# Four sequence-matrix blocks split on TensorE, and a re-ordered half-step plan, in an attention + Fourier kernel on one core

## The chip, the core and the metric

The kernel runs on one core of a Trainium2 chip. The metric is the device time of one execution in microseconds (us). The engines are named as in the profile: PE is TensorE's matmul row and PEld its weight loads, DVE is VectorE, ACT is ScalarE, POOL is GpSimd, and SP is SyncE, which here only issues DMAs.

## What is computed

Four layers over one sequence of S = 2048 rows of D = 640 numbers, each added to its input: attention, Fourier mixing, attention, Fourier mixing. The reference, cut to what matters (`idx` is the row minus 0, 2, ..., 14, and negative rows are masked):

```python
def _A_ref(x, wqkv, wo):                      # 32 heads of 20
    qkv = (x @ wqkv).reshape(B, S, 3, H, Dh)  # -> q, k, v
    kg, vg = k[..., idx, :], v[..., idx, :]   # 8 rows per query, 2 apart
    logits = einsum("bhsd,bhswd->bhsw", q, kg) * scale
    attn = softmax(where(mask, logits, -1e9))
    o = einsum("bhsw,bhswd->bhsd", attn, vg)
    return o.reshape(B, S, D) @ wo
def _B_ref(x, seq_re, seq_im, hid_re, hid_im):
    a, b = x @ hid_re.T, x @ hid_im.T
    return seq_re @ a - seq_im @ b
x = x + _A_ref(layernorm(x), wqkv, wo)
x = x + _B_ref(layernorm(x), ...)
x = x + _A_ref(layernorm(x), wqkv, wo)
x = x + _B_ref(layernorm(x), ...)
```

All arrays are fp32. Since the matmuls take a rounded form (fp32r), every operand is split into a high part and a low part, `low = x - high`, and each product is the sum of three: high by high, high by low, low by high (`PASSES`).

## The kernel before

**Layers and pieces.** `layer_a` is an attention layer (called with 0 and 2; the text says first and second attention layer), `LayerB` a Fourier layer. The rows are permuted on the host, even ones first, and stand in four chunks (c = 0 to 3) of four tiles of 128 rows (j = 0 to 3). The attention layers also do a part of the Fourier layer behind them: the product of the sequence matrix's first block column with the normalized rows, `z_mm`, in sixteen blocks (block 4c + j needs tile j of chunk c), each in three thirds of five matmuls.

**Half-steps.** Heads are taken four at a time; a unit u (0 to 31) is four heads of one chunk, and each unit has two halves. One half is one half-step s, numbered from about -8 to 66. In half-step s = 2u + jp VectorE multiplies q with the windows of k (`qk_mul`, L518), GpSimd adds the two halves of each head's 20 products (L521), VectorE sums the remaining ten (`qk_red`, L531). A half-step in `whole` leaves GpSimd's addition out, and VectorE sums all twenty. Then follow the softmax pieces (`soft`, L546 to L556, in phases sA to sF), with `exp` on ScalarE (L539) between the subtraction sC and the sum sD; three half-steps after its `qk_mul`, VectorE multiplies with v (`av_mul`, L561), and GpSimd adds over the 8 rows (`av_tree`, L576 to L578).

**The plan.** Every call of a layer is entered in a plan under a half-step and a phase, and the plan is played half-step by half-step in the order of the phases in `ph`, one string for s < 48 and one for the rest:

```python
for s in range(gs[0], last + 1):
    for ph in C["ph"][s >= 48].split():
        for fn, args in plan.pop((s, ph), ()):
            fn(*args)
```

Each engine executes its own instructions in this written order, and a wait holds up all that follows on that engine. SyncE's DMA queue is such an order too. The numbers in CFG are half-steps: `gs` for the 64 groups of QKV matmuls, `wo` for the output projection, `z` for the thirds of `z_mm`, `ln` for the normalization, `t2`, `t3` for transposes of the attention output.

**What the change touches.**
- Sequence blocks. `c_load` loads block z (128x512) into a `stg` buffer, `c_hi` (L985) copies its high part on ScalarE, `c_lo` (L1001) subtracts on VectorE, `c_put` stores both for the second attention layer. `zla` is by how many half-steps a block is prepared earlier, `cring` the ring of its tiles, here `s3`, `s0`, `s2`.
- Transposes. `tp` enters one for tiles of x or of the attention output in four phases: `peT0` (`pc_pe`, L414, matmuls with the identity into a PSUM bank), `hi` (`pc_hi`, L418, ScalarE copies the rounded high part out), `peL` (`pc_sub`, L422, a matmul with minus the identity subtracts the high part in the bank) and `actL` or `loE` (`pc_lo`, L437, ScalarE copies the low part out).
- `q_load` (L488) loads a unit's q into a `qs` buffer two half-steps ahead; `q_copy` (L491) moves it on ScalarE into the PSUM tile `pq` that `qk_mul` reads. There is one `qs` buffer. `w_load` (L504) loads the windows of k and v.
- `qkv_mm` (L449), `qkv_evac` (L456, out of PSUM into a `stg` buffer) and `qkv_store` (L465, L466) make k, v and q and store them. `stg` has two buffers, shared with the blocks.
- `wo_mm` (L601) is the output projection into the banks `aux0` and `aux1`, `wo_add` (L237) adds its result to the residual on VectorE. `ln_hi` and `ln_lo` (L955, L959) split the normalized rows; `lnv` tells whether `ln_lo` is on VectorE (1) or GpSimd (0).
- `wqg` tells which low halves of the QKV weights (`split`, L212) GpSimd forms in the first layer.

Of the kernel before, what the change touches and what calls it, by code (L numbers as in the profile page):

```python
# [21 lines left out]
H = 32  # L22
# [14 lines left out]
CFG = {'cput': [1, 1, 1, 1, 1, 1, 1, 1, 1, 1, 1, 1, 1, 1, 1, 1],  # L37
# [12 lines left out]
 'run': [{'pre': [0, 0, 0, 0, 0, 0, 0, 1, 0, 0, 0, 4, 0, 0, 0, 0],  # L50
          'post': [1, 5, 4, 2, 3, 3, 2, 6, 3, 1, 0, 3, 1, 3, 3, 3],
          'y': [[6, 6, 6, 6, 6], [13, 13, 16, 16, 16]]},
         {'pre': [0, 0, 0, 0, 0, 6, 0, 0, 2, 0, 0, 0, 0, 0, 0, 0],
          'post': [0, 4, 4, 5, 0, 2, 1, 1, 0, 5, 6, 0, 5, 1, 6, 0],
# [5 lines left out]
         'ord': [[2, 0, 1, 3, 4, 6, 5, 7], [0, 2, 1, 3, 4, 6, 5, 7], [0, 2, 1, 3, 4, 6, 5, 7]],  # L60
         'out': [20, 24, 28, 32, 36, 40, 44, 46],
         'wo': [23, 23, 26, 27, 30, 30, 34, 35, 37, 38, 42, 43, 46, 47, 49, 49],
         'woph': 'pe2',
# [4 lines left out]
         'z': [149, 149, 151, 151, 151, 152, 152, 154, 155, 161, 163, 163, 170, 170, 170, 172, 173, 173, 174, 175,  # L68
               176, 176, 177, 178, 180, 182, 182, 182, 185, 185, 185, 186, 186, 188, 191, 191, 191, 191, 194, 195,
# [7 lines left out]
         'kvq': [1, 1, 0, 0, 0, 0, 0, 0, 0, 0, 0, 0, 0, 0, 0, 0, 0, 0, 0, 0, 0, 0, 0, 0, 0, 0, 0, 0, 0, 0, 0, 0],  # L77
# [12 lines left out]
         'whole': [33, 57],  # L90
         'lnv': [1, 0, 1, 1, 0, 1, 0, 0, 0, 0, 0, 0, 1, 1, 0, 0]},
# [4 lines left out]
         'ord': [[0, 2, 1, 3, 4, 6, 5, 7], [2, 0, 1, 3, 4, 6, 7, 5], [0, 2, 1, 3, 4, 6, 5, 7]],  # L96
         'out': [20, 25, 29, 32, 36, 41, 44, 46],
         'wo': [22, 23, 28, 28, 30, 31, 34, 35, 38, 39, 42, 43, 46, 47, 48, 49],
         'woph': 'z1',
         'ln': [42, 42, 44, 46, 52, 54, 55, 56],  # L100
         'w2': [52, 53, 54, 55],
# [49 lines left out]
def tile_layers(ctx: ExitStack, tc: tile.TileContext, x, wqkv, wo, cs, wre, wim, out):  # L151
# [175 lines left out]
    def layer_a(li, stats, handoff, prev):  # L327
# [376 lines left out]
        def prologue_first():  # L704
# [27 lines left out]
            for k in range(3):  # L732
                whi(k, nc.scalar)
# [3 lines left out]
            for i in range(2):  # L737
                xt_pe(0, 0, i, f"t{i}")
# [707 lines left out]
```

## Time and profile before

| | |
|---|---|
| three runs | 1776.55, 1783.21, 1781.76 us; median 1781.76 |
| profiled execution | 1776.27 us; span on the core 1774.5 us |
| mean granted TensorE clock | 0.995 |
| first attention layer | from the start to about 411 us |
| second attention layer | from about 876 to about 1281 us |
| the two Fourier layers | what lies between, and after, to the end |

A line of the busy times by stage names the stretch, its length, then for each engine the busy us and the count of instructions. A line of the waits reads: engine and what it was about to do, `<-` what it waited for, then us in total, times, longest. A line of the groups has line, engine, operation, output `<-` inputs, shape and count, then busy us and mean ns of one, then idle time before them. A line of the timeline has start, duration, and the same names, with the idle time before it in brackets.

### The profile page before, as it was taken

Reading aid. Unit: us, or ns where it says so; the run is one execution under the profiler, and the core shown is the slowest. Engines: PE = TensorE matmul, PEld = TensorE weight load, DVE = VectorE, ACT = ScalarE, POOL = GpSimd, SP = SyncE. Lnnn points to the kernel's source line nnn. Section 1 sums busy time; section 2 is a strip of 40 time slices with the busy share of each in tenths; the row PEclk is TensorE's granted clock in tenths of the full one; section 3 lists DMA queues with packets and bytes.
Section 4 is the critical chain, followed back from the end, with each engine's and each line's share of the span. In section 5 each row is a group of like instructions: output and inputs, shape, how many; then the busy total and the mean of one; then the engine's idle time right before and its main releaser. Section 6 shows DMA issues by size and latency. Waiting matters only on the chain.

```text
span 1774.5 us, 26375 instructions
## 1 busy us (share of the span) xinstructions
PE 1727.7 (97%) x8798; PEld 1503.3 (85%) x8798; DVE 1369.2 (77%) x2124; ACT 812.1 (46%) x1700; POOL 625.7 (35%) x577
## 2 busy tenths in 40 slices
PE   9999998899999999999999999999999999999999
PEld 6878987777888888888898889888788888888888
DVE  5899899977767768668639987898877677677673
ACT  5554644544445445445533434444534443443441
POOL 3799898970000000000019987898300000000000
PEclk9999999999999999999999999999999999999999
DMA  6786668868777687687647856688688776867761
GB/s 231 233 279 208 202 205 276 279 245 292 269 268 234 219 268 239 208 273 231 220 143 244 260 175 215 204 303 289 206 296 276 260 231 224 269 224 235 257 210 52
DMA packets 266312, 419.38 MB, mean 236 GB/s; under 512 B 22176, under 2 KB 146592, under 8 KB 265920
## 3 DMA queue, kind: packets, MB, share of 16 engines
q1 hardware_dynamic: 262976, 415.72, 70.9%
q10 hardware_dynamic: 3200, 1.97, 0.4%
q8 instruction: 70, 1.15, 0.3%
q14 instruction: 66, 0.54, 0.1%
HBM read 332.46 MB, written 85.14 MB: 235 GB/s over the span
## 4 chain that ended last, share of the span: by engine, by line
PE 71%; DVE 13%; DMA 9%; issue 3%; ACT 2%; POOL 1%; SPq 1%; DVEq 0%; ACTq 0%; POOLq 0%
PE m L449 19%; PE aux L1090 13%; PE t L1189 10%; PE m L1189 10%; PE pq L1189 5%; PE xt L1189 5%; PE aux L601 5%; DMA xc<-stg 3%; DVE pr L518 2%; DMA win<-cs_in 2%; DVE pr L561 1%; DMA win<-kvb 1%; DVE lg L531 1%; DVE stg L1155 1%; DVE s L1001 1%
## 5 line engine op out<-in xcount | busy, mean ns | idle before, releaser
L449 PE MATMUL m<-r,s 128*128 128x480 f32 x1920 | 434.5, 381 | 4.1 <-ACT s L437 1.7
L449 PEld LDWEIGHTS m<-r,s 128*128 128x128 f32 x1920 | 355.0, 188 | 58.2 <-ACT stg L456 3.3
L1090 PE MATMUL aux<-r2a,zo 128*128 128x320 f32 x768 | 226.0, 309 | 0.0
L1182 ACT CAST r<-win 128x512 fp32r<-128x512 f32 x242 | 147.5, 621 | 171.2 <-DVE win L1218 84.8
L576 POOL TENSOR_TENSOR pr<-pr 128x640 f32<-128x640 f32 x126 | 209.2, 1660 | 31.3 <-DVE pr L561 30.0
L518 DVE TENSOR_TENSOR pr<-pq,win 128x1280 f32<-128x1280 f32 x128 | 189.8, 1483 | 35.4 <-ACT pq L491 17.1
L521 POOL TENSOR_TENSOR pr<-pr 128x640 f32<-128x640 f32 x126 | 180.1, 1429 | 100.7 <-DVE pr L518 100.4
L1090 PE MATMUL aux<-pr,zo 128*128 128x320 f32 x704 | 207.9, 309 | 0.0
L1183 DVE TENSOR_TENSOR r<-win,r 128x512 fp32r<-128x512 f32 x242 | 162.8, 686 | 42.0 <-ACT r L1182 40.9
L561 DVE TENSOR_TENSOR pr<-pq,win 128x1280 f32<-128x1280 f32 x128 | 190.7, 1490 | 4.1
L259 POOL TENSOR_TENSOR stats<-stats,mhalf 128x1 f32<-128x1 f32 (+1 forms) x32 | 23.2, 724 | 465.8 <-ACT stats L253 465.8
L1189 PE MATMUL m<-r,r 128*128 128x512 f32 x600 | 153.0, 389 | 0.1
L1090 PEld LDWEIGHTS aux<-r2a,zo 128*128 128x128 f32 x768 | 144.2, 188 | 1.9
L1090 PEld LDWEIGHTS aux<-pr,zo 128*128 128x128 f32 x704 | 132.2, 188 | 2.1
L1189 PEld LDWEIGHTS m<-r,r 128*128 128x128 f32 x600 | 112.4, 188 | 23.6 <-DVE r L1183 0.5
L1189 PE MATMUL t<-r,r 128*128 128x512 f32 x492 | 132.0, 390 | 0.0
L1016 PE MATMUL m<-s,r 128*128 128x512 f32 x384 | 121.2, 402 | 8.9 <-DVE r L959 3.5
L1016 PE MATMUL t<-s,r 128*128 128x512 f32 x384 | 118.2, 396 | 2.2 <-DVE ot L1069 1.3
L577 POOL TENSOR_TENSOR pr<-pr 128x320 f32<-128x320 f32 x126 | 114.3, 907 | 9.9
L456 ACT COPY stg<-m 128x480 f32<-128x480 f32 x128 | 71.2, 556 | 90.6 <-PE m L449 74.8
L531 DVE TENSOR_REDUCE lg<-pr 128x64 f32<-128x640 f32 (+1 forms) x128 | 104.4, 815 | 7.3 <-POOL pr L521 7.0
L1189 PEld LDWEIGHTS t<-r,r 128*128 128x128 f32 x492 | 92.4, 188 | 19.8
(274 smaller groups left out, 3206.1 us busy)
## 6 DMA issues: line engine op xcount, KB each, us to landing
win<-cs_in SPq DMA_DIRECT2D x346, 256.0 KB, 4.1
r<-xc SPq DMA_DIRECT2D x240, 256.0 KB, 4.3
win<-kvb SPq DMA_DIRECT2D x96, 440.0 KB, 5.0
xa<-cs_in SPq DMA_DIRECT2D x120, 256.0 KB, 3.8
win<-kvb SPq DMA_DIRECT2D x64, 360.0 KB, 4.8
xc<-stg SPq DMA_DIRECT2D x40, 512.0 KB, 3.3
kvb<-stg SPq DMA_DIRECT2D x60, 320.0 KB, 4.1
xr<-xs SPq DMA_DIRECT2D x40, 320.0 KB, 4.9
```

The source lines that it names most:

```text
L449: nc.tensor.matmul(mt[g][:, : 3 * F], st[:, a, k], wq[q][:, b, k], start=n == 0, stop=n == 14)
L518: nc.vector.tensor_tensor(pr, q, wview(u, jp, 0, [[1, FE]]), op=ALU.mult)
L521: nc.gpsimd.tensor_tensor(pv[:, :, 0:10], pv[:, :, 0:10], pv[:, :, 10:20], op=ALU.add)
L531: nc.vector.tensor_reduce(rows(lgs[u], jp), pv.rearrange("p (a h) d -> p a h d", h=HE), axis=AX.X, op=ALU.add,)
L561: nc.vector.tensor_tensor(pr.rearrange("p j w (h d) -> p (j w) h d", d=DH), rows(lgs[u], jp).unsqueeze(3).to_broadcast([P, 2 * W, HE, DH]) ...
L576: g.tensor_tensor(pr[:, :, 0:4], pr[:, :, 0:4], pr[:, :, 4:8], op=ALU.add)
L577: g.tensor_tensor(pr[:, :, 0:2], pr[:, :, 0:2], pr[:, :, 2:4], op=ALU.add)
L1016: self.last = nc.tensor.matmul(self.z[t][k], self.xn[c][:, a, j, k * P : (k + 1) * P], self.ct[s][:, b], start=s == 0 and i == 0, stop=s = ...
L1090: self.last = nc.tensor.matmul(self.ym[e][:, :320], zt[(k, a, ri)][:, j2 * P : (j2 + 1) * P], w[:, e * 320 : (e + 1) * 320], start=(k, a, ...
L1182: nc.scalar.copy(hi, raw)
L1183: nc.vector.tensor_tensor(lo, raw, hi.bitcast(F32), op=ALU.subtract)
L1189: nc.tensor.matmul(bank, w(a, kb), hl[b], start=start and (a, b) == (0, 0), stop=stop and (a, b) == (1, 0),)
```

## The change

Four of the sixteen blocks (8, 9, 10 and 12, by `cpe`) are loaded in the first attention layer from a copy of the matrix that the host has transposed, 128x128 piece by piece. They go through the four phases of a transpose instead of `c_hi` and `c_lo`: TensorE transposes the pieces into `aux0` or `aux1`, ScalarE copies the high part out, TensorE subtracts it, ScalarE copies the low part out. The ring of block tiles in that layer gets a fourth tile, `wa`. `qs` gets a second buffer, `stg` a third.

The plan's numbers are set anew. In the first 48 half-steps sC now stands ahead of av0 (`av_mul`) in both layers; in the second layer `red1` also stands ahead of sD. Block copies and `ln_lo` have phases of their own (`clo`, `lnl`) instead of `misc`, and several thirds of `z_mm` move by a half-step or to another phase, in the first layer in front of the `peL` of half-steps 52, 57, 58, 59 and 61, in the second in front of those of 50, 52 and 59. `whole` gets two more half-steps in each layer. In the first layer two `ln_lo` move to VectorE, in the second one moves to GpSimd; eight instead of four weight splits are GpSimd's; five pairs of k, v and q stores are issued by ScalarE instead of two. The start of the first layer is written as a string of steps (`pro`), in nearly the same order. `lnx` and the calls of `z_late` change no instruction here.

By count, TensorE gets 16 transposes and 4 subtracting matmuls more, ScalarE 4 copies more, VectorE 4 subtractions of 128x512 fewer, GpSimd 4 first additions fewer. 

The diff, cut:

```diff
- 'bufs': {'xa': 2, 'qs': 1, 'stg': 2, 'xr': 1},
+ 'bufs': {'xa': 2, 'qs': 2, 'stg': 3, 'xr': 1},
- 'wqg': [0, 0, 0, 0, 0, 0, 0, 0, 1, 0, 0, 1, 0, 0, 0, 0, 1, 1, 0, 0],
+ 'wqg': [0, 0, 0, 0, 0, 1, 0, 1, 1, 1, 0, 0, 0, 1, 0, 0, 1, 1, 1, 0],
...
  first attention layer:
-         't2': [48, 48, 47, 48, 52, 52, 52, 51],
+         't2': [48, 48, 48, 48, 51, 51, 52, 51],
-         'kvq': [1, 1, 0, 0, ...],
+         'kvq': [1, 0, 0, 1, 0, ..., 1 at 16, 26 and 30],
-         'cring': ['s3', 's0', 's2'],
-         'zla': [0, 0, 0, 0, 0, 0, 0, 0, 0, 0, 0, 0, 0, 0],
-         'ph': ['peT0 pe dma evac hi z1 z0 peL pe2 fin red0 dma2 qk sA sB av0 sD sE red1 sC loE exp evacA actL actl '
-                'sF evacO av1 qc dmaw dmas misc dmac dmar pe3w pe3',
-                'peT0 dma hi evac z0 pe peL pe2 z1 fin red0 dma2 qk sA av0 sD sB red1 sE loE sC actL exp evacA actl '
-                'sF evacO dmac av1 qc dmas misc dmar dmaw pe3 pe3w'],
+         'cring': ['s3', 's0', 'wa', 's2'],
+         'cpe': [0, 0, 0, 0, 0, 0, 0, 0, 1, 2, 2, 0, 2, 0],
+         'zla': [0, 0, 0, 0, 0, 0, 0, 0, 0, 0, 1, 0, 1, 0],
+         'ph': ['peT0 pe dma evac hi z1 fin z0 peL pe2 red0 qk sA dma2 sB sC av0 sD sE red1 loE exp actl evacA sF '
+                'actL evacO av1 qc dmaw pe3w dmas misc lnl clo dmac dmar pe3',
+                'peT0 evac dma hi z0 peL pe pe2 z1 red0 fin dma2 qk sA av0 sD sB red1 sE loE sC actL exp evacA sF '
+                'evacO dmac dmar av1 qc misc lnl clo dmas dmaw pe3 pe3w'],
-         'whole': [33, 57],
-         'lnv': [1, 0, 1, 1, 0, 1, 0, 0, 0, 0, 0, 0, 1, 1, 0, 0]},
+         'whole': [7, 19, 27, 57],
+         'lnv': [1, 1, 1, 1, 0, 1, 0, 0, 0, 1, 0, 0, 1, 1, 0, 0]},
...
  second attention layer:
-         't3': [59, 58, 60, 61],
+         't3': [59, 58, 60, 60],
-         'ph': ['peT0 dma evac hi z0 pe peL pe2 z1 fin red0 dma2 sA qk sD sB av0 red1 sE sC loE exp evacA actL actl '
-                'sF evacO av1 dmaw dmas qc misc dmar pe3w pe3 dmac',
+         'ph': ['peT0 dma evac hi red0 pe z0 peL qk z1 fin sA sB pe2 red1 dma2 sD sE evacA sC av0 loE exp actL actl '
+                'sF evacO av1 qc dmaw misc lnl clo dmas dmar pe3w pe3 dmac',
-         'whole': [],
+         'whole': [51, 55],
...
             if first:
                 la = C["zla"][z]
-                at(t - 2 - la, "dmac", handoff.c_load, z)
-                at(t - 1 - la, "hi", handoff.c_hi, z)
-                at(t - 1 - la, "misc", handoff.c_lo, z)
+                if C["cpe"][z]:
+                    tp(t - 1 - la, "c", 0, z, 0, 4, f"aux{C['cpe'][z] - 1}")
+                    at(t - 2 - la, "dmac", handoff.ct_load, z)
+                else:
+                    at(t - 2 - la, "dmac", handoff.c_load, z)
+                    at(t - 1 - la, "hi", handoff.c_hi, z)
+                    at(t - 1 - la, "clo", handoff.c_lo, z)
...
+        def ct_load(self, s):
+            self.raw[s] = T([P, 512], "stg", bufs=CFG["bufs"]["stg"])
+            nc.sync.dma_start(self.raw[s], cst[:, s, :])
+
+        def ct_new(self, s):
+            self.ct[s] = T([P, 2, 512], self.c_tag(s), F32R)
+            return self.raw[s], self.ct[s].rearrange("p a (k f) -> p a k f", f=P)
...
+    cst = np.ascontiguousarray(cs[0].reshape(P, NST, 4, P).transpose(3, 1, 2, 0).reshape(P, NST, 512))
```

The numbers of `gs`, `ord`, `out`, `wo`, `ln`, `z`, `early` and `run` change in places too, mostly by one half-step.

More of the change, by code (lines that the diff above doesn't have):

```diff
@@ L116 @@
          'cring': ['s3', 's0', 's2'],
[L117 to L121 removed]
+         'cpe': [0, 0, 0, 0, 0, 0, 0, 0, 0, 0, 0, 0, 0, 0],
@@ L150, in tile_layers @@
 @with_exitstack
-def tile_layers(ctx: ExitStack, tc: tile.TileContext, x, wqkv, wo, cs, wre, wim, out):
+def tile_layers(ctx: ExitStack, tc: tile.TileContext, x, wqkv, wo, cs, cst, wre, wim, out):
     nc = tc.nc
@@ L402, in pc_pe @@
                     (xnT if kind == "x" else oT)[(c, j, 1) if kind == "x" else (c, j)] = T([P, 2, KD, P], tag, F32R)
-                src, st = (
+                if kind == "c":
+                    src, st = handoff.ct_new(j)
+                else:
+                    src, st = (
                         (xnT[(c, j)], xnT[(c, j, 1)]) if kind == "x" else (oo[(c, j // 2)][:, j % 2], oT[(c, j)])
@@ L408, in pc_pe @@
                 pb, todo = banks[bank]
+                assert not todo or (kind != "c" and todo[-1][0].offset != pb.offset + col)
                 todo += [(pb[:, col + i * P : col + (i + 1) * P], src[:, k * P : (k + 1) * P]) for i, k in enumerate(range(k0, k1))]
@@ L853, in layer_a @@
                 else:
-                    tp(C["t3"][j] if j < 2 else TA, "o", c, j, 0, 3, f"aux{j % 2}", 0, ("ot", "s1", "zo0", "zo1")[j])
+                    tp(C["t3"][j] if j < 2 else TA, "o", c, j, 0, 3, f"aux{j % 2}", 0, (["ot", "s1"] + [CFG["zor"][(4 + x) % len(CFG["zor"])] for x in range(2)])[j])
                     tp(C["t3"][2 + j] if j < 2 else 67, "o", c, j, 3, 5, "aux0" if j < 2 else "pq", 256 * (j % 2))
@@ L882, in layer_a @@
         assert len(thirds) == 42
+        late = {}
         for z in range(len(thirds) // 3):
@@ L894, in layer_a, with z_late @@
             for p in range(3):
-                at(*thirds[3 * z + p], handoff.z_mm, z, p)
+                if thirds[3 * z + p][0] > last:
+                    late.setdefault(thirds[3 * z + p][0], []).append((z, p))
+                else:
+                    at(*thirds[3 * z + p], handoff.z_mm, z, p)
+        def z_late(t):
+            for z, p in late.pop(t, ()):
+                handoff.z_mm(z, p)
         with tc.manual_schedule(engines=ENGINES):
@@ L929, in layer_a @@
             handoff.z_mm(15, None)
-        assert not plan, plan.keys()
+        assert not plan and not late, (plan.keys(), late)
         return nstats
```

120 lines of the change are left out of this document (67 added, 53 removed), and 14 rows, old and new, of the table CFG.

## The prediction

> **What bounds the kernel now.** I read the page first, then the busy time by stage, then the waits of TensorE, VectorE and SyncE's queue inside the two attention layers.
>
> ```profile
> span 1774.5 us, 26375 instructions
> PE 1727.7 (97%) x8798; PEld 1503.3 (85%) x8798; DVE 1369.2 (77%) x2124; ACT 812.1 (46%) x1700; POOL 625.7 (35%) x577
> PE 71%; DVE 13%; DMA 9%; issue 3%; ACT 2%; POOL 1%; SPq 1%; DVEq 0%; ACTq 0%; POOLq 0%
> ```
>
> TensorE is busy 97% of the span and carries 71% of the chain. Averages hide the stages, so next the busy time in stretches (PE, PEld, DVE, ACT, POOL, then the granted clock, the DMA share and GB/s):
>
> ```profile
> 60.00:276.00 216.00, 210.84 (x1090) 186.03 (x1090) 199.54 (x287) 115.93 (x290) 199.30 (x185) 1.00 0.71 228
> 276.00:340.00 64.00, 52.77 (x285) 45.69 (x283) 59.19 (x88) 31.99 (x81) 55.61 (x51) 0.95 0.82 283
> 340.00:386.00 46.00, 41.27 (x191) 34.52 (x192) 43.58 (x60) 19.39 (x44) 42.57 (x37) 0.93 0.84 293
> 386.00:411.00 25.00, 21.39 (x107) 17.80 (x105) 14.31 (x29) 13.32 (x30) 5.09 (x5) 0.93 0.57 195
> 411.00:917.00 506.00, 503.54 (x2557) 440.17 (x2558) 357.03 (x584) 242.97 (x457) 5.62 (x6) 1.00 0.72 240
> 917.00:1146.00 229.00, 226.82 (x1174) 201.58 (x1173) 199.06 (x284) 90.26 (x218) 192.28 (x177) 1.00 0.70 221
> 1146.00:1262.00 116.00, 109.25 (x586) 94.20 (x585) 103.36 (x157) 56.08 (x140) 100.63 (x88) 1.00 0.78 268
> 1281.00:1774.00 493.00, 488.72 (x2487) 426.57 (x2485) 343.12 (x557) 198.10 (x343) 0.00 (x0) 1.00 0.70 230
> ```
>
> The two transform layers (411 to 917 and 1281 to 1774) keep TensorE busy for all but 2.5 and 4.3 us; the change hardly touches them, and I give them nothing. In the first attention layer TensorE is full until 276 and then idles 11.2 us (64.00 - 52.77), 4.7 us and 3.6 us in the next three stretches, at a granted clock of 0.95 and 0.93. In just those stretches VectorE idles only 4.8 us of 64 and 2.4 us of 46, and GpSimd is nearly as full. So the first layer's late part is paced by the VectorE/GpSimd attention chain, and TensorE waits for its products. The second attention layer is TensorE's until 1146; then it idles 6.8 us to 1262. What the change can win lies here: 24.7 us of TensorE idle from 60 to 411 and 8.9 us from 917 to 1262, not the 3% of the whole.
>
> What TensorE waits for from 276 to 411, then what VectorE waits for (60 to 386, then 917 to 1262), then the longest wait of SyncE's queue in either layer:
>
> ```profile
> PE aux L422 <- ACT s L418: 4.0, 3, 2.9
> PE aux L414 <- POOL pr L576: 3.2, 1, 3.2
> PE m L1016 <- DVE r L959: 2.5, 1, 2.5
> PE aux L422 <- ACT ot L418: 1.7, 1, 1.7
> ...
> DVE pr L518 <- ACT pq L491: 6.8, 5, 3.6
> DVE lg L531 <- POOL pr L521: 4.0, 7, 0.8
> DVE pr L518 <- DMA win<-kvb: 2.3, 3, 0.9
> ...
> DVE pr L518 <- ACT pq L491: 7.1, 5, 2.7
> DVE lg L546 <- ACT pq L491: 5.8, 4, 3.0
> ...
> SPq L488 <- ACT pq L491: 43.1, 11, 5.9
> ...
> SPq L488 <- ACT pq L491: 37.5, 12, 6.0
> ```
>
> VectorE's largest wait in both layers is for `q_copy` (L491) on ScalarE, and SyncE's queue stands 43.1 and 37.5 us behind `q_load` (L488), whose single `qs` buffer is free only after that copy.
>
> **The change part by part, first layer.** The four low halves (blocks 8, 9, 10 and 12) leave VectorE. In the trace they are the 9th, 10th, 11th and 13th of the fourteen `c_lo` from `stg`:
>
> ```profile
> 348.04 3.51 DVE L1001 TENSOR_TENSOR s<-stg,s 128x512 fp32r<-128x512 f32 x2
> ...
> 355.64 0.72 DVE L1001 TENSOR_TENSOR s<-stg,s 128x512 fp32r<-128x512 f32 x1
> ...
> 368.67 0.81 DVE L1001 TENSOR_TENSOR s<-stg,s 128x512 fp32r<-128x512 f32 x1
> ```
>
> 3.51 + 0.72 + 0.81 = 5.0 us, all where VectorE paces (its idle there is 2.4 of 46 us): **-5.0**.
>
> In their place come, per block, four transposes and one subtracting matmul on TensorE, and one more copy out of PSUM on ScalarE; a `c_hi` that read `stg` now reads PSUM. The nearest rows:
>
> ```profile
> L414 PE MATMUL xt<-ident,xa 128*128 128x128 f32 x96 | 14.4, 272 | 0.0
> L422 PE MATMUL xt<-s,nident 128*128 128x512 f32 x24 | 9.7, 403 | 3.2 <-ACT s L418 3.2
> L1189 PE MATMUL m<-r,r 128*128 128x512 f32 x600 | 153.0, 389 | 0.1
> L437 ACT CAST s<-xt 128x512 fp32r<-128x512 f32 x24 | 14.1, 589 | 2.8 <-PE xt L422 2.8
> ```
>
> A transpose occupies TensorE for 14.4 / 96 = 0.15 us, sixteen for 2.4 us; a subtraction for between 153.0 / 600 = 0.26 and 9.7 / 24 = 0.40 us, four for 1.0 to 1.6 us. Together 3.4 to 4.0 us in half-steps 59 to 61, where TensorE has 4.7 us idle. Half on the path: **+1.8** (0 if the idle takes all of it, +4.0 if that idle is gone). The mean of one transpose in the same row, 272 ns, is start to end of overlapping instructions. The Trainium skill (TensorE: Matmul & The Clock Gate, Part 4) gives about 275 ns for a transpose in a kernel; priced one after another at that figure, sixteen would be an estimated 4.4 us and the sum 1.0 us worse. The group's busy time decides for 0.15. The four ScalarE copies are 4 x 0.59 = 2.4 us, and ScalarE is busy 19.39 of 46 us: at nothing, or 2.4 us if they stand ahead of an `exp`.
>
> Block 12's transposes add a wait: their bank `aux1` is the one that `wo_mm` of chunk 3 fills in half-step 60, and `wo_add` empties it only at the end of half-step 61, so everything on TensorE queues behind it.
>
> ```profile
> 353.98 4.56 PE L601 MATMUL aux<-r2a,ot 128*128 128x320 f32 x30
> ...
> 361.19 0.48 DVE L237 SCALAR_TENSOR_TENSOR xa<-aux,xa 128x320 f32<-128x320 f32 x1
> ```
>
> TensorE is through with that product at 358.5 and `wo_add`'s first half ends at 361.7: 3.2 us of stall if nothing else moved. But three of the four removed `c_lo` (4.2 us) stand ahead of it on VectorE, so I cost it at **0**; 3.2 is the price without that cover.
>
> The softmax subtraction now stands ahead of `av_mul` in the first 48 half-steps, so `exp`, which blocks ScalarE's queue, is fed one `av_mul` earlier and `q_copy`, last in that queue, comes sooner: of the 6.8 us I take 2: **-2.0** (0 to -6.8). The second `qs` buffer ends SyncE's stand at L488, so window loads go out earlier: **-1.5** of the 2.3 us for windows. What is late next on that queue is the stores' wait for their evacuation, which is unchanged. The third `stg` buffer unties the block loads from earlier `c_lo`; counted within these.
>
> Layer normalisation's low halves: two more on VectorE, two fewer on GpSimd. `whole`: four half-steps instead of two skip GpSimd's first addition. One of either kind:
>
> ```profile
> L959 DVE TENSOR_TENSOR r<-r,r 128x640 fp32r<-128x640 f32 x5 | 5.4, 1073 | 0.0
> L959 POOL TENSOR_TENSOR r<-r,r 128x640 fp32r<-128x640 f32 x11 | 17.3, 1571 | 0.0
> L531 DVE TENSOR_REDUCE lg<-pr 128x64 f32<-128x640 f32 x126 | 101.4, 805 | 7.3 <-POOL pr L521 7.0
> L531 DVE TENSOR_REDUCE lg<-pr 128x64 f32<-128x1280 f32 x2 | 3.0, 1476 | 0.0
> ```
>
> VectorE gets 2 x 1.07 and GpSimd loses 2 x 1.57 us; as both are full I take half: **+1.0**. Two reductions longer by 1.476 - 0.805 are +1.3 us, against the 4.0 us that VectorE waits for GpSimd's L521 in seven places of about 0.6 us, some of them in half-steps 7 and 19, now `whole`: **-0.3**. Four weight splits moved to GpSimd lie before 60 us and at nothing.
>
> Half-steps 52, 57, 58 and 61 now have a third of a sequence product, or one more, between TensorE's transposes and the subtraction that waits for ScalarE (the waits on L418 above, 4.0 + 1.7). That only fills idle time of an engine that follows the chain: it is counted as what lets TensorE keep up, at 0. Half-step 60 loses such a filler.
>
> First layer: -5.0 + 1.8 - 2.0 - 1.5 + 1.0 - 0.3 = **-6.0 us**.
>
> **Second layer.** No block moves. VectorE's 12.9 us of waits on L491 (7.1 + 5.8) shrink by the same reorder and buffer, but until 1146 TensorE is full (226.82 of 229), so the gain can only appear as less of its 6.8 us idle to 1262: **-3.0**. One transpose group no longer waits for a `wo_add` that follows it, and half-steps 50, 52 and 59 get fillers: **-1.0**. Two more `whole` (+1.3) and one low half off VectorE (-1.07): +0.2. Together **-3.8 us**.
>
> The sum is -9.8 us: 1776.3 us (the profiled execution: span 1774.5 and 1.8 around it) becomes 1766.5. The three runs shown stand at 1776.6, 1781.8 and 1783.2; the mean of all four is 1779.5, 3.2 above the profiled one. For the median of new runs I add that: about **1769 us**.
>
> **Rivals.** *Everything goes* (chance 0.24): all of the waits on L491 and for windows in the first layer (-9.1 instead of -3.5), the added matmuls wholly in idle time (0 instead of +1.8), and the second layer's 6.8 us idle gone (-7 instead of -3.8): 10.6 us better, 1759. For: the waits are named and the buffers are what they wait for. Against: TensorE is full until 276, so what VectorE wins earlier shows only if TensorE's next wait is for VectorE.
>
> *TensorE covers it* (0.16): the reorder moves who waits, both layers keep their pace, and only -5.0 + 4.0 + 1.0 remain: 1779, no change. For: 210.84 of 216 us. Against: 24.7 us idle in that layer.
>
> *TensorE's clock falls* (0.13, the slower one). Where TensorE stood still for 3.2 us, at 291 to 295, the granted clock was halved after it:
>
> ```profile
> 291.07 0.61 PE L1016 MATMUL t<-s,r 128*128 128x512 f32 x2
> 294.88 0.45 PE L414 MATMUL aux<-ident,zo 128*128 128x128 f32 x1 [3.21 <-POOL pr L576]
> ...
> 297.79 1.06 PE L1016 MATMUL m<-s,r 128*128 128x512 f32 x2
> ```
>
> Two matmuls take 0.61 us before it and 1.06 us after it. By the granted clocks of the stretches the loss is 0.05 x 64 + 0.07 x 46 + 0.07 x 25 = 8.2 us already. If the stall at half-step 61 (3.2 us) comes and the emptier queue at 51, two thirds of a product fewer than before, lengthens that one, halved stretches double (+8.2) and none of the -9.8 but the 5.0 arrives: -5.0 + 4.0 + 3.2 + 8.2 = +10.4, 1790. It decides as soon as block 12 waits over 3 us for `wo_add`. The Trainium skill (same page, Part 1) says that an idle window of about 3.4 us halves the clock, and Part 4 that transposes do not count as activity; by that rule this layer, with sixteen more, would lose more clock. The halved stretch after 3.2 us agrees.
>
> *It does not do what it says* (0.05): `q_load` still waits, now for the stores to `qb`, and the reorder is undone by ScalarE's queue: without -2.0, -1.5 and -3.0, 1776.
>
> **How the numbers follow.** The forecast has 0.42, 1762 to 1774 by its own bounds. About 0.5% is what a measurement of this kernel can tell from no change; around the mean of 1779.5 these are 1771 and 1788. Faster: 0.24 and 0.27 of the forecast = 0.51. Same: the other 0.15 of it, 0.16 and 0.05, less 0.04 for the slow ends of those two = 0.32. Slower: 0.13 + 0.04 = 0.17. The range reaches down to 1751, everything-goes with the 8.2 us of lost clock back as well, and up to 1788; left out is the clock case at its full price and what little lies below.
>
> **What would show it.** Right: VectorE's L1001 from `stg` x10 instead of x14, the end of the first layer's full VectorE stretch before 382 instead of at 386, the waits L518 on L491 halved, SyncE's L488 waits gone, and TensorE's idle from 276 to 340 under 9 us. Wrong: a TensorE wait over 2 us ahead of the block transposes, a granted clock under 0.93 there, or an unchanged end of the first layer near 411.

## The result, and the profile after

The changed kernel takes 1763.14 us (median of 4 runs, 1762.23 to 1763.97) where the kernel before takes 1779.97 (1776.55 to 1783.21): a ratio of 0.9906, with a 95% interval of 0.9884 to 0.9927. The profiled execution takes 1763.97 us (before: 1776.27), so the two traces differ by 12.3 us in their spans and the medians by 16.8: the profiled execution of before was among the fastest of its kernel. The forecast was 1769 us, and the time lies on the side that was forecast and inside the range; most of the reasons behind the forecast were not the ones that the chip shows.

The head of the page after: its span and the busy times.

```profile
span 1762.2 us, 26348 instructions
PE 1727.8 (98%) x8818; PEld 1507.3 (86%) x8818; DVE 1366.8 (78%) x2117; ACT 814.1 (46%) x1704; POOL 621.8 (35%) x576
```

TensorE's busy time is what it was (1727.7 before) although it has 20 matmuls more, and VectorE has lost no more than 2.4 us. The kernel is shorter because TensorE stands still less. The busy time in stretches (PE, PEld, DVE, ACT, POOL, granted clock, DMA share, GB/s):

```profile
60.00:276.00 216.00, 213.22 (x1101) 188.07 (x1100) 199.11 (x283) 113.58 (x283) 195.26 (x182) 1.00 0.69 225
276.00:340.00 64.00, 57.01 (x298) 49.21 (x297) 61.91 (x93) 35.65 (x86) 58.30 (x52) 0.95 0.93 327
340.00:386.00 46.00, 41.13 (x215) 35.23 (x214) 36.43 (x52) 18.75 (x45) 35.35 (x32) 0.96 0.64 225
386.00:411.00 25.00, 21.29 (x98) 17.34 (x99) 17.64 (x34) 15.30 (x34) 4.97 (x4) 0.93 0.62 208
411.00:917.00 506.00, 504.96 (x2577) 442.30 (x2576) 354.72 (x579) 239.73 (x453) 6.50 (x7) 1.00 0.74 241
1146.00:1262.00 116.00, 111.02 (x600) 96.11 (x599) 104.21 (x161) 57.33 (x143) 95.33 (x84) 1.00 0.80 274
```

TensorE's idle time from 276 to 340 is 7.0 us instead of 11.2, and VectorE and GpSimd are no longer full from 340 to 386: VectorE idles 9.6 of 46 us there instead of 2.4. To see where the 12.3 us come from, one point of the program is looked up in both timelines: the last four transposes of an attention layer, which start in the first and in the second layer at (start in us, duration; before first, then after)

```profile
388.50 0.60 PE L414 MATMUL pq<-ident,zo 128*128 128x128 f32 x4
1259.74 0.60 PE L414 MATMUL pq<-ident,zo 128*128 128x128 f32 x4
```

```profile
384.78 0.60 PE L425 MATMUL pq<-ident,zo 128*128 128x128 f32 x4
1248.80 0.60 PE L425 MATMUL pq<-ident,zo 128*128 128x128 f32 x4
```

and, as a point some 90 us into the second layer, the fourth set of transposes of x that it puts into the bank `xt`, before and after:

```profile
973.87 0.60 PE L414 MATMUL xt<-ident,xa 128*128 128x128 f32 x4
```

```profile
969.23 0.60 PE L425 MATMUL xt<-ident,xa 128*128 128x128 f32 x4
```

So the first attention layer gives 3.7 us (388.50 - 384.78), the way from there to the point in the second layer another 0.9 (4.6 in all at 969), the rest of the second attention layer 6.3 (10.9 in all at 1249), and what lies behind it 1.4. Each trace is one execution, and the runs of one kernel lie some us apart: such a difference is that of two executions.

The waits after: TensorE from 276 to 411, VectorE from 60 to 386, VectorE from 917 to 1262, SyncE's queue from 60 to 386 (us in total, times, longest).

```profile
PE aux L433 <- ACT s L429: 4.3, 2, 2.1
PE aux L425 <- POOL zo L589: 2.0, 1, 2.0
PE m L1055 <- DVE r L990: 1.7, 1, 1.7
...
DVE pr L529 <- ACT pq L502: 11.2, 11, 2.4
DVE lg L542 <- POOL pr L532: 1.7, 4, 0.8
...
DVE pq L563 <- ACT lg L550: 10.5, 6, 2.7
DVE pr L529 <- ACT pq L502: 3.7, 6, 1.4
...
SPq L476 <- ACT stg L467: 49.2, 13, 10.2
```

The wait of VectorE for `q_copy` (L491 before, L502 now) has grown in the first layer, from 6.8 to 11.2 us, and moved to `exp` (L550) in the second. SyncE's queue hardly stands at `q_load` any more (3.7 us); it stands 49.2 us at the stores of the evacuated pieces instead.

### The profile page after: what moved, and what is told of

Read it like the earlier page. It is cut to its first block, busy times and chain, and to the rows that moved or that the text cites. A ratio compares the mean times of both kernels' runs of the same rounds, so it can differ in the third digit from the quotient of the medians.

```text
span 1762.2 us, 26348 instructions
## 1 busy us (share of the span) xinstructions
PE 1727.8 (98%) x8818; PEld 1507.3 (86%) x8818; DVE 1366.8 (78%) x2117; ACT 814.1 (46%) x1704; POOL 621.8 (35%) x576
## 4 chain that ended last, share of the span: by engine, by line
PE 88%; DMA 4%; DVE 4%; ACT 2%; issue 1%; POOL 0%; SPq 0%; ACTq 0%; DVEq 0%
PE m L460 24%; PE aux L1129 15%; PE t L1228 10%; PE m L1228 10%; PE aux L612 6%; PE pq L1228 5%; PE xt L1228 5%; PE t L1055 4%; PE m L1055 4%; PE xt L1055 2%; DMA win<-cs_in 1%; DMA win<-kvb 1%; DMA stg<-cs_in 1%; PE t L425 1%; PE xt L425 1%
## 5 line engine op out<-in xcount | busy, mean ns | idle before, releaser
L587 POOL TENSOR_TENSOR pr<-pr 128x640 f32<-128x640 f32 x126 | 208.7, 1657 | 44.9 <-DVE pr L572 43.8
L532 POOL TENSOR_TENSOR pr<-pr 128x640 f32<-128x640 f32 x122 | 174.9, 1433 | 85.4 <-DVE pr L529 84.9
L1055 PE MATMUL m<-s,r 128*128 128x512 f32 x366 | 114.9, 402 | 6.2 <-DVE r L990 2.6
L1055 PE MATMUL t<-s,r 128*128 128x512 f32 x366 | 113.4, 398 | 2.3 <-DVE ot L1108 1.4
L1257 DVE TENSOR_TENSOR win<-win,win 128x512 f32<-128x512 f32 x109 | 74.8, 689 | 49.2 <-DMA win<-cs_in 47.8
```

The lines of the kernel that those rows point to most:

```text
L532: nc.gpsimd.tensor_tensor(pv[:, :, 0:10], pv[:, :, 0:10], pv[:, :, 10:20], op=ALU.add)
L587: g.tensor_tensor(pr[:, :, 0:4], pr[:, :, 0:4], pr[:, :, 4:8], op=ALU.add)
L1055: self.last = nc.tensor.matmul(self.z[t][k], self.xn[c][:, a, j, k * P : (k + 1) * P], self.ct[s][:, b], start=s == 0 and i == 0, stop=s = ...
```

## Experiments

Three theories stood against each other at first. By the prediction VectorE's path is shorter (the low halves, the softmax order, the earlier windows). By the second, TensorE's order in the two attention layers makes the gain (which thirds of a sequence product stand where TensorE would wait). By the third, the buffers make it. Each run was timed against the kernel before on the same chip, in five rounds; the ratios have 95% intervals.

**The buffers without the plan.**

```diff
- 'bufs': {'xa': 2, 'qs': 1, 'stg': 2, 'xr': 1},
+ 'bufs': {'xa': 2, 'qs': 2, 'stg': 3, 'xr': 1},
```

> The kernel before with two qs and three stg buffers and nothing else. VectorE-path theory: the waits for windows and half of those on q_copy go, 3 to 6 us below before, SyncE's waits at L488 under 10 us per layer. TensorE-order theory: within 2 us of before. Buffer theory: 10 us or more below.

Measured: 1772.23 us against 1781.38, 0.9954 [0.9943, 0.9966]. Two numbers give half of the whole gain. Which of the two it is, two more runs tell.

> The kernel before with one number changed: three stg buffers instead of two (qs stays at one). The stg ring holds the evacuated query/key/value pieces and the raw sequence-matrix blocks of the attention layers, but also the pairs of split halves that the Fourier layers store (L1151). In the kernel before VectorE waits there for the store to leave its stg buffer (L1153, 2.8 and 2.5 us near 482 and 1353 us) and TensorE then for ot (1.85 and 1.35 us over its pitch). Theory A (this ring is what the buffers bring): 3.2 us from these two places and 2 to 4 us in the attention layers, so 5 to 7 us faster, about 1775, and both Fourier stalls gone. Theory B (the prediction: the qs buffer is the one that frees the window loads, the stg buffer is a means): under 2 us, and the Fourier stalls stay.

> The kernel before with two qs buffers instead of one (stg stays at two). Theory A (the stg ring brings most of it): SyncE's wait at L488 goes, its queue then stands at the stores' wait for their evacuation (L465) instead, and the time moves by 0 to -3 us. Theory B (the prediction): the windows come earlier, -1.5 us in the first layer and as much of the second layer's idle, so -3 to -4 us, and the two Fourier stalls stay under both. If the two buffers alone each bring much less than both together (9.2 us), they gate one another on SyncE's queue.

The third `stg` buffer alone: 1772.19 against 1780.02, 0.9960 [0.9948, 0.9971]. The second `qs` buffer alone: 1779.13, 0.9993 [0.9984, 1.0002]. It is `stg`, and SyncE's long stand at `q_load` cost little or nothing (by the interval, its end lies between 2.8 us faster and 0.4 us slower): in the run with the third `stg` and a single `qs` the queue still stands there for as long as before, and the run is as fast as the one with both buffers within the intervals. In the run with the second `qs` alone that stand is gone and the queue stands at the next entry. Its trace reaches the first layer's last transposes 2.4 us earlier than before's (386.06), but of that 0.1 us is left at the point in the second layer (973.76). The waits of SyncE's queue from 60 to 386, `stg` run first, `qs` run second:

```profile
SPq L488 <- ACT pq L491: 42.1, 12, 5.9
SPq L465 <- ACT stg L456: 17.9, 10, 5.8
```

```profile
SPq L465 <- ACT stg L456: 55.6, 15, 6.2
```

Part of what `stg` gives lies where the prediction gave nothing. The Fourier layers put their split halves into the same ring (L1151) before they store them. In the kernel before VectorE waits there for the store to leave the buffer, and TensorE then for VectorE (waits from 411 to 917, then from 1290 to the end):

```profile
DVE stg L1153 <- DMA xc<-stg: 7.1, 6, 2.3
PE t L1189 <- DVE ot L1072: 1.7, 1, 1.7
...
DVE stg L1153 <- DMA xc<-stg: 9.9, 9, 2.3
PE t L1189 <- DVE ot L1072: 1.2, 1, 1.2
```

With the third buffer VectorE's wait is down to these (the second stretch from 1285 here, from where before has 10.4 us), and neither of TensorE's two rows is left:

```profile
DVE stg L1153 <- DMA xc<-stg: 3.1, 4, 1.6
...
DVE stg L1153 <- DMA xc<-stg: 3.1, 4, 1.1
```

TensorE's 2.9 us are gone in the changed kernel as well. The rest of the 7.8 us is not carried by any single wait in these traces, and the two traces end only 4.1 us apart (1774.5 and 1770.4): 1.4 us of it are there at the first layer's last transposes (387.09), 1.3 at the second's (1258.45), and 2.8 come behind those, where the last Fourier layer lies. The Trainium skill (Perfetto Trace Analysis, Optimization Strategy) says that the same gap coming again and again on the engine that should be saturated can mean that there is no room for the next tile, the number of buffers being one cause that it names. Here such a gap stood on VectorE, which is not saturated (busy 357 of 506 us), and a buffer more made it smaller (17.5 to 6.2 us from 411 to 917 and from 1285).

**The four blocks without the rest** (the kernel before with its own buffers and half-steps, but block 12 one half-step earlier, and the phases `lnl` and `clo` behind `misc` as in the changed kernel).

```diff
+ 'cpe': [0, 0, 0, 0, 0, 0, 0, 0, 1, 2, 2, 0, 2, 0],   # first layer
- 'cring': ['s3', 's0', 's2'],
+ 'cring': ['s3', 's0', 'wa', 's2'],
- 'zla': [0, 0, 0, 0, 0, 0, 0, 0, 0, 0, 0, 0, 0, 0],
+ 'zla': [0, 0, 0, 0, 0, 0, 0, 0, 0, 0, 0, 0, 1, 0],
- ... qc dmaw dmas misc dmac ...           # ph, here s < 48
+ ... qc dmaw dmas misc lnl clo dmac ...
```

> The kernel before with blocks 8, 9, 10 and 12 through TensorE (block 12 one half-step earlier, the ring with the tile wa), old plan and old buffers. VectorE-path theory: -5.0 on VectorE and +1.8 on TensorE, about 3 us below before. TensorE-order theory: no gain, 0 to 4 us above before, since the added transposes stand on the old plan without fillers and block 12 waits for wo_add. Buffer theory: within 2 us.

Measured: 1786.14, 1.0032 [1.0019, 1.0044], slower. The waits of TensorE from 276 to 411 show one for the load of the transposed copies into `stg`, which the kernel before does not have:

```profile
PE aux L425 <- DMA stg<-cst_in: 2.2, 2, 1.3
```

If the ring is what makes the blocks a loss, a third buffer ends it:

> The kernel before with the four blocks formed on TensorE, as in the run of the blocks alone (5.7 us slower than before there), and now with three stg buffers. Alone, the third stg buffer gave 7.8 us (1772.2 against 1780.0). Theory A (the blocks lost because a transposed copy holds its stg buffer until TensorE comes to its transposes; TensorE waited 2.2 us for the loads into stg): with the third buffer the loss is gone, 1771 to 1774. Theory C (the transposes and the extra bank cost TensorE themselves on the order of before): the loss stays, 1776 to 1779. The prediction (VectorE's pace, -5.0 + 1.8): 3 us faster than the third buffer alone, about 1769.

Measured: 1774.86, 0.9965 [0.9953, 0.9977], the same as the third buffer alone (0.9960) within the intervals, and that wait is down to

```profile
PE aux L425 <- DMA stg<-cst_in: 1.0, 2, 0.7
```

The loss is gone, and no gain comes in its place. But the two runs do more than move four blocks: with `lnl` and `clo`, VectorE does some additions of the output projection ahead of low halves of the normalization (near 256, 276 and 316 us). The run of the second layer's plan further down has this order in its first layer too, with both buffers and no block, and is later there than the run of the buffers alone (the last four transposes of the first layer, buffers alone first):

```profile
385.93 0.60 PE L414 MATMUL pq<-ident,zo 128*128 128x128 f32 x4
```

```profile
390.16 0.60 PE L425 MATMUL pq<-ident,zo 128*128 128x128 f32 x4
```

So how much of the loss of the blocks alone (4.8 us by the medians, 5.7 by the ratio, beside a wait of 2.2) is theirs, and how much that order's, isn't told by these runs, and neither is what the blocks are worth on the old order. The third question on the blocks is what they do inside the changed kernel:

```diff
- 'cpe': [0, 0, 0, 0, 0, 0, 0, 0, 1, 2, 2, 0, 2, 0],
+ 'cpe': [0, 0, 0, 0, 0, 0, 0, 0, 0, 0, 0, 0, 0, 0],
```

> The kernel after with the four blocks back on VectorE (c_hi from stg, c_lo from stg and s), all else as after. The prediction's step: +5.0 on VectorE, -1.8 on TensorE, so 3.2 us slower than after, about 1766. Theory A (the buffers and the order brought what the kernel after gained, and VectorE's and GpSimd's slack covers the four low halves now: VectorE idles 9.6 of 46 us from 340 to 386): within 1.5 us of after either way. Theory C (the blocks are a loss here too, as alone on the old order, where they cost 5.7 us): 3 to 6 us faster than after.

Measured: 1763.53, 0.9905 [0.989, 0.992], against 0.9906 [0.9884, 0.9927] with the blocks. The intervals alone would leave room for some 5 us either way, so the trace is asked: its stretch from 340 to 386, and the start of the last four transposes of the first layer.

```profile
340.00:386.00 46.00, 38.50 (x189) 32.43 (x189) 41.73 (x57) 17.97 (x42) 37.93 (x33) 0.93 0.68 236
```

```profile
384.80 0.60 PE L425 MATMUL pq<-ident,zo 128*128 128x128 f32 x4
```

The blocks do exactly what they say: with them VectorE has 5.3 us less to do in this stretch (36.43 against 41.73) and TensorE 2.6 us more (41.13 against 38.50). The layer gets to its last transposes at 384.78 with them and at 384.80 without, and at the two later points the traces are 0.2 us apart (969.23 and 1248.80 with, 969.04 and 1249.03 without). TensorE's waits for VectorE from 276 to 411 are 5.5 us with the blocks and 5.7 without, none of them for a block's low half. The work taken off VectorE came off an engine that did not pace, and what TensorE got was put into its own idle time: 7.5 us without the blocks, 4.9 with them.

**One layer's plan at a time**, both with the new buffers. In the first run the second layer's entries of `ly` and `run` are those of before; in the second run it is the first layer's, without the blocks and with the prologue of before. The old layer has the phases `lnl` and `clo` in both.

> The change in the first attention layer alone: the second layer has its old plan, both have the new buffers. VectorE-path theory (the prediction's): first layer -6.0 us and part of the second layer's -3.0 through the buffers, so about 7 us below before. TensorE-order theory (fillers and half-steps of the sequence thirds): the change's trace is 3.7 us ahead at the end of the first layer and 8.4 us more by the end of the second Fourier layer, so about 4 to 6 us below before. Buffer theory: nearly all of the 12 to 17 us, as the buffers serve both layers.

> The change in the second attention layer alone, with the new buffers in both layers; no block goes through TensorE. VectorE-path theory: -3.8 us of the second layer and 2 to 4 us through the buffers in the first, about 6 below before. TensorE-order theory: the second layer's fillers carry 6 to 8 us. Buffer theory: nearly all of the 12 to 17 us again.

Measured: 0.9942 [0.993, 0.9955] with the new first layer, 0.9938 [0.9926, 0.995] with the new second layer, against 0.9954 [0.9943, 0.9966] with the buffers alone. Each plan alone gives 2 to 3 us more, within the intervals; both together bring the ratio to 0.9906, 8.5 us (0.0048 of 1780) below the buffers. Whether the two add is not settled by the times: what is left over, some 3.5 us, is no larger than the intervals. The traces say where to look. Between the two points of the second layer 279.5 us pass with its new plan alone (975.94 to 1255.45), as in the changed kernel (279.6), and 287.0 with the buffers alone (970.12 to 1257.12): that layer's gain comes with its own plan. The old layers lose meanwhile, 4.2 us in the second run's first layer (390.16 against 385.93) and 2.3 us between the two points in the first run (289.3 against 287.0), so each plan looks smaller alone than it is.

**What in the plan counts.** First the fillers: the thirds of sequence products that stand between the second transposes and the subtraction that waits for ScalarE's copy. In the changed kernel's plan for half-steps 48 and later, in both layers, the phase `z0` goes behind `peL`. That takes out the new fillers and also those that the kernel before had.

```diff
-'peT0 evac dma hi z0 peL pe pe2 ...     # first layer
+'peT0 evac dma hi peL z0 pe pe2 ...
-'peT0 evac dma red0 z0 hi pe peL pe2 ...  # second layer
+'peT0 evac dma red0 hi pe peL z0 pe2 ...
```

> The kernel after with the thirds of sequence products (phase z0) back behind the second transposes' subtraction (peL) in the last half-steps of both attention layers, where the kernel before had most of them. The prediction counted these fillers at 0 in the first layer and -1.0 with another edit in the second. By the prediction: at most 1 us slower than after. Theory D (the fillers are what keeps TensorE running past ScalarE's copy): the waits of L433 on ScalarE's copy L429 come back, 2 to 5 us slower than after, 1765 to 1768.

Measured: 1769.77 (1766.0 to 1771.99), 0.9939 [0.9926, 0.9952], 6.6 us above the changed kernel (5.9 by the ratios, whose intervals just touch; no run of it is as fast as the slowest of the changed kernel). In the first layer (276 to 411) TensorE's waits of L433 for ScalarE's copies of `s`, `zo` and `ot` (L429) have grown from 4.5 us to the 8.4 us of three rows below, the wait for a bank that VectorE empties (L244) has grown from 1.3 us, and the last transposes come 7.0 us later:

```profile
PE aux L433 <- ACT s L429: 4.9, 4, 2.6
PE aux L425 <- DVE xa L244: 2.3, 1, 2.3
PE aux L433 <- ACT zo L429: 2.2, 1, 2.2
...
PE aux L433 <- ACT ot L429: 1.3, 1, 1.3
```

```profile
391.73 0.60 PE L425 MATMUL pq<-ident,zo 128*128 128x128 f32 x4
```

Then the softmax's place, back behind `av0` in the first 48 half-steps of both layers:

```diff
-'... qk sA dma2 sB sC av0 sD sE red1 loE ...   # first layer
+'... qk sA dma2 sB av0 sD sE red1 sC loE ...
-'... sE evacA sC av0 loE ...                   # second layer
+'... sE evacA av0 sC loE ...
```

> The kernel after with the softmax subtraction (phase sC) of the first 48 half-steps back behind av_mul (av0), in both layers. The prediction took 2.0 us in the first layer (0 to 6.8) and most of 3.0 us in the second for this and the buffer: 3 to 5 us slower than after, 1766 to 1768, and more wait of VectorE for q_copy (L502) than after's 11.2 us from 60 to 386. The other theory: in after's trace those waits are not smaller than before (11.2 against 6.8 us), and TensorE is full until 276 in the first layer and until 1146 in the second, which is where these half-steps lie; then the place is worth within 1 us of after, 1762 to 1764.

Measured: 1764.34, 0.991 [0.9897, 0.9922], 1.2 us above the changed kernel's median and not to be told from it. VectorE's waits for `q_copy` from 60 to 386 are no larger in the old place (11.2 in the new one):

```profile
DVE pr L529 <- ACT pq L502: 10.7, 9, 2.6
```

The traces leave room for a small gain by the new place. In the old one the first layer's last transposes come 4.0 us later (row below, against 384.78) and the second's 2.6 us (1251.41 against 1248.80); the spans end only 0.3 us apart, but the granted clock from 1262 to 1281 was 1.00 with the old place and 0.91 in the changed kernel.

```profile
388.81 0.60 PE L425 MATMUL pq<-ident,zo 128*128 128x128 f32 x4
```

Then more of what counted. Three thirds move one phase earlier, to `z0`: one each in half-steps 58 and 60 of the first layer, one in half-step 58 of the second.

```diff
- ... 173, 174, 174, 175, 175, 175, 176, 177, 181, 182 ...   # z, first layer
+ ... 173, 174, 174, 174, 175, 175, 176, 177, 180, 182 ...
- ... 171, 171, 173, 175, 176, 177 ...                       # z, second layer
+ ... 171, 171, 173, 174, 176, 177 ...
```

> The kernel after with three thirds of sequence products moved one phase earlier, ahead of the second transposes' subtraction: in the first layer one in half-step 58 (from phase z1 to z0, beside the two that are there) and the one of half-step 60 (z1 to z0), in the second layer one in half-step 58. In after's trace TensorE stands 2.3 us at each of the two places of the first layer and 0.7 us in the second, and a third of a product is about 1.4 us. Theory D (fillers ahead of ScalarE's copy are what the new order gains by): 1.4 + 1.4 + 0.7, up to 3.5 us faster than after, 1760 to 1762. The prediction (an engine that follows the chain has only its idle time filled): no change, 1763.

Measured: 1759.31 (1757.52 to 1760.97), 0.9874 [0.9859, 0.9889]. No run of it is as slow as the fastest of the changed kernel (1762.23), although the two intervals touch. It is the fastest version here. The wait for ScalarE's copy in the first layer is less than half of what it was (4.3), and the layer's last transposes come 2.4 us earlier:

```profile
PE aux L433 <- ACT s L429: 1.9, 2, 1.6
```

```profile
382.39 0.60 PE L425 MATMUL pq<-ident,zo 128*128 128x128 f32 x4
```

Of the 3.6 us between the two traces (spans 1762.2 and 1758.6) 1.9 are there at the second layer's last transposes (1248.80 and 1246.92), and all of it comes from the first layer: the third moved in the second layer changes nothing between its two points (279.57 and 279.55 us). The other 1.7 us come behind, where the granted clocks differ (last section).

At last, whether the third buffer and the new half-steps of the thirds make the change without the rest: the kernel before with `stg` 3 and the two `z` lists of after.

> The kernel before with two things of the change alone: three stg buffers, and the half-steps of the thirds of sequence products (the lists z of both layers) as in the kernel after, so that half-steps 57, 58 and 61 of the first layer have a third ahead of the second transposes' subtraction. No block on TensorE, one qs buffer, every other half-step as before. The third buffer alone stood at 0.9960 of before, the kernel after at 0.9906, the kernel after without its fillers at 0.9939. Theory D (the ring and the fillers are nearly all of it, and they add): 0.9960 less 0.0033, so 0.9925 to 0.993, about 1767. Rival E (fillers gain only where the rest of the half-steps' order is the new one, which has the copies and the loads of the blocks in other places): 0.995 to 0.997, 1773 to 1776, as the third buffer alone.

Measured: 1774.96, 0.9969 [0.9956, 0.9982], as the third buffer alone: the theory that fillers and ring add up fell. On the old order TensorE's waits of L422 for ScalarE's copies from 276 to 411 are 6.2 us before and already down to 1.8 with the third buffer alone, so there was little left to fill. With the new half-steps they are 2.6, GpSimd's last sums cost 5.1 (7.0 in two rows with the buffer alone), and a wait for a bank that VectorE has to empty comes new:

```profile
PE aux L414 <- POOL zo L578: 5.1, 3, 1.8
PE aux L414 <- DVE xa L237: 3.6, 1, 3.6
PE aux L422 <- ACT s L418: 2.1, 2, 1.2
```

A reading that no run shows by itself: a filler gains only where nothing else ends just behind it, and the new order is one in which the bank and the sums are nearly in time (1.3 and 2.0 us there).

## Why the prediction was right or wrong

The time was right: 1769 was forecast, 1763.14 came, inside the range; as a sum against its own execution -9.8 us were forecast and the traces show -12.3. Of the terms few held, and misses of both signs made up for each other.

- *First layer, -6.0.* The traces show -3.7; that of the buffers alone already shows -2.6 (385.93).
- *The low halves, -5.0 on VectorE and +1.8 on TensorE.* Both amounts of work came true (5.3 us off VectorE; the sixteen transposes were priced at 2.4 us, and their row after is below), and the time did not: the layer reaches its last transposes 0.02 us earlier than without them. The step that failed is "all where VectorE paces". VectorE is full there, but with 5.3 us taken off it TensorE's waits for VectorE are 5.5 us instead of 5.7, those for ScalarE the same 6.4, and only those for GpSimd fall (6.4 to 3.6), by about the work that TensorE gets. A full engine beside an idle TensorE was taken for the one that sets the pace. Besides, its busy time is in part waiting: a low half takes 0.68 us by itself, four 2.7, and the rest of the 5.0 was spent behind GpSimd's instructions (last section).

```profile
L425 PE MATMUL aux<-ident,stg 128*128 128x128 f32 x16 | 2.2, 272 | 0.0
```

- *The softmax's place, -2.0.* The wait that it was to shorten grew in the whole change (6.8 to 11.2 us), and the place does not set it (10.7 with the old one). In the time the place is worth 1.2 us and not told from nothing; one trace has more (4.0 us at the first layer's last transposes), so the mechanism failed and the size is open. The half-steps it touches lie where TensorE is full, which was what stood behind the rival *TensorE covers it*.
- *The second `qs` buffer, -1.5 and part of the second layer's -3.0.* 0.9993 [0.9984, 1.0002] alone. The stand of SyncE's queue at L488 is gone as forecast, but what it held up was not late. The stores' wait behind it was called unchanged; it grew from 18.9 us to 55.6.
- *The third `stg` buffer, "counted within these".* This is the largest miss: alone, on the old order, it gives 7.8 us, nearly half of the change. Only its use for the block loads was priced. That the Fourier layers take their staging from the same ring, where a store holds it, was not looked up; *Fourier layers: nothing* failed with it, if only by the 0.9 and 1.4 us that the traces of before and after show around those parts.
- *Fillers, at 0.* Their place is worth up to 6.6 us in the new order (with those that before had), nothing in the old one, and 3.8 us more with three further ones (1.9 in the traces without the last stretch, where the clocks differ). "An engine that follows the chain" was said to have only its idle time filled; here the same thirds otherwise stand behind the wait, on TensorE's own path, and the layer ends later.
- *Second layer, -3.8.* The traces show -6.3. `q_copy`'s 12.9 us of waits became 3.7 plus 10.5 at `exp`, so the named mechanism is not it. The fillers account for 1.9 of it: without them the two points of that layer are 281.5 us apart (rows below), with them 279.6 (969.23 to 1248.80). The remainder goes with the new order of that layer, as its plan alone shows (279.5 us), and was not taken apart.

```profile
977.37 0.60 PE L425 MATMUL xt<-ident,xa 128*128 128x128 f32 x4
...
1258.87 0.60 PE L425 MATMUL pq<-ident,zo 128*128 128x128 f32 x4
```

- *The stall at half-step 61 at 0, wq splits at 0, low halves of the normalisation and `whole` at +1.0 and -0.3.* Block 12's four transposes start at 358.11 us behind no wait, so the cover held. The others were not tried alone, so the sum of the first layer can't be followed term by term.
- *Rivals.* The clock stayed where it was (0.95, 0.96 and 0.93 in the three late stretches, 0.95, 0.93 and 0.93 before), although the layer has sixteen more transposes. By the Trainium skill (TensorE: Matmul & The Clock Gate, Part 4) these do not count as activity; the loss of clock that the rule would give did not come. *Everything goes* (1759) was nearer to the time than the forecast, for other reasons than its own. *It does not do what it says* had the worth of `qs` and of the softmax's place about right, but not its reason: `q_load` hardly waits any more.
- *What would show it.* Ten `c_lo` from `stg` instead of fourteen, SyncE's waits at `q_load` gone and TensorE's idle from 276 to 340 under 9 us (7.0) came true; the waits for `q_copy` halved and VectorE's full stretch ended before 382 did not (in the changed kernel it is busy 3.96 of the 5 us from 380 to 385). Three true signs stood beside a wrong cause: they showed that the edits had taken place, not that they paid.

How much of the 16.8 us is accounted for: 7.8 by the `stg` ring, if it is worth in the new order what it is in the old one (the changed kernel with two `stg` buffers was not run); nothing that could be told from 0 by the blocks and by `qs`; the other 9, by subtraction, by the new order of the two layers, in which the fillers' place, with those that before had, carries up to 6.6. Which edits of that order make the fillers work there and not on the old order is open.

## What to carry to other kernels

A full engine next to an idle TensorE is a suspect, not the bound: look at what TensorE's own waits name, and ask what frees that. Before a ring of buffers is made longer, look up every stage that takes from it, since a ring that is roomy in one layer can be what a store holds up in another. Work without a deadline belongs in front of an in-order engine's wait for another engine's copy, and its value there can only be judged together with what ends next behind it.

## What the runs showed of the hardware

The turn out of the second attention layer (1262 to 1281) ran at a granted clock of 0.91 in the profiled execution of the changed kernel and at 1.00 in that of the one with more fillers, whose last part is the same (rows below). It was 0.91 without the blocks and 1.00 with the softmax's old place, which have that last part too. By estimate 0.09 of 19 us is 1.7 us, which is what is left of the 3.6 us between the first two traces after the second layer's last transposes. What decides between the two clocks isn't shown.

```profile
1262.00:1281.00 19.00, 16.90 (x66) 13.13 (x67) 16.55 (x27) 11.25 (x21) 0.00 (x0) 0.91 0.76 258
```

```profile
1262.00:1281.00 19.00, 17.25 (x75) 13.38 (x74) 17.93 (x28) 11.10 (x21) 0.00 (x0) 1.00 0.77 258
```

The same subtraction of the same shape on VectorE, a block's low half, took from 0.68 to 2.05 us in the changed kernel, and which of these it took follows GpSimd's timeline (VectorE first, then GpSimd):

```profile
299.70 1.56 DVE L1040 TENSOR_TENSOR s<-stg,s 128x512 fp32r<-128x512 f32 x1
330.31 0.68 DVE L1040 TENSOR_TENSOR wa<-stg,wa 128x512 fp32r<-128x512 f32 x1
330.91 2.05 DVE L1040 TENSOR_TENSOR s<-stg,s 128x512 fp32r<-128x512 f32 x1
```

```profile
299.30 1.42 POOL L532 TENSOR_TENSOR pr<-pr 128x640 f32<-128x640 f32 x1
330.69 1.72 POOL L587 TENSOR_TENSOR pr<-pr 128x640 f32<-128x640 f32 x1
```

At 299.70 GpSimd's instruction has 1.02 us to go, and the subtraction takes 1.56; at 330.91 it has 1.50 to go, and the subtraction takes 2.05; at 330.31 no such instruction has begun, and it takes 0.68. So the subtraction ends about 0.55 us after the GpSimd instruction that was running at its start. In the traces of seven of the kernels here (264 to 420 us) this holds for each of the 42 subtractions listed singly that began behind a GpSimd instruction (0.54 to 0.56 us after its end; GpSimd's operations on the few numbers of `stats` do not count), and each of the 60 others took 0.68 or 0.69 us. VectorE's busy time in these layers thus holds time in which a subtraction did not go on before GpSimd had ended, which no list of waits shows.
